# Second layer's begin in a two-layer decode kernel: where the rest of a kept V is put, and the order of the requests behind it

## The chip, the core and the metric

One core of a Trainium2 chip runs the whole program. The metric is the time on the device in microseconds (us), the median of several runs; a profiled execution gives a trace with the span and the records of each engine: PE (matmuls), DVE, ACT, POOL, SP (SyncE, which here only asks for transfers), and the 16 DMA engines.

## The reference

One token passes attention with a cache of 4096 positions and an MLP, and the same two blocks once more with the same weights and caches.

```
def _A_ref(x, k_cache, v_cache, wq, wo):
    q = (x @ wq) as 32 heads of 128
    scores = einsum("bhqd,bhkd->bhqk", q, k_cache) * (Dh ** -0.5)
    p = softmax(scores)
    o = einsum("bhqk,bhkd->bhqd", p, v_cache)
    return o @ wo                      # wq 512 x 4096, wo 4096 x 512

def _B_ref(x, w1, b1, w2, b2):
    return gelu(x @ w1 + b1) @ w2 + b2 # 512 -> 1376 -> 512

x = x + A(layernorm(x));  x = x + B(layernorm(x))
x = x + A(layernorm(x));  x = x + B(layernorm(x))
```

All is float32. K and V are 64 MiB each and are read in both layers, except for what is kept.

## The kernel before

The 32 heads are taken in 8 groups of four (`G`, `J`). A group's K is 8 MiB, in 8 chunks of 1 MiB (`C`); a chunk is 2048 columns (`NC`) of the 128 partitions. V is cut likewise. One tile, `arena` (line 74), holds nearly everything; places in it are told here in slots of `NC` columns, 0 to 27. Slots 0 to 23 take three blocks of 8 MiB in turn; `SPARE` is slot 19.75, `HELD` 22.75, `PAIR` 25.44 (two chunks: a wo and a wq). A `load` (line 76) is one request on SP's queue; the requests stay in the order of the program, and each waits until the last readers of its place are done. SP runs them one after the other, so a waiting one holds all behind it.

The first layer takes the groups 0 to 7, the second 7 to 0, so the second layer starts with data that are still there. Call its first three turns of the loop (line 380, n = 0, 1, 2; groups 7, 6, 5) stage one, two and three, with K7, V7, K6, V6, K5, V5.

A stage: `scores` (line 199; 4 MATMULs a chunk, which the trace shows as 8 passes), `softmax` (line 204: DVE takes the maximum, ACT the exponential, PE turns the result at line 213), `values` (line 227; 8 passes a chunk), `scaled_out` (line 232), `head_out` (line 254, the product with wo), `queries` (line 188: DVE four steps at lines 190 and 192, PE four products at line 194). `idle` (line 356) is a filler: a MATMUL whose result nobody reads. Fillers stand before the change in the last stage of each layer (`FILL` = 3 behind the scores and some more) and in the MLP.

What lies where when the second layer begins:

- K7 in slots 0 to 7, V7 in 8 to 15, all there.
- V6's first 3.75 chunks in slots 16 to 19.75, and 1.25 more in five PSUM banks (`pK`). The rest, 3 MiB, was overwritten by weights and is loaded again.
- K6 goes to `SPARE` + 1 and + 2 (chunks 0, 1), `PAIR` + 1 (chunk 2), and slots 0 (chunk 3) and 1 to 4 (chunks 4 to 7, one request), as K7's chunks are scored.
- V6's chunks 3 to 7 are put together in slots 6 to 10: its rest is loaded to slots 8 to 10 once V7's chunks there are used, and ACT copies the kept part to slots 6 and 7 (lines 413, 416).
- The weights of the next stages go to `PAIR`; then K5 in two halves to slots 12 to 15 and 16 to 19; then V5 to 0 to 7.
- Stage one's softmax writes to slot 5 (`p`), and the turned values (`ot`) right behind it (`free_now`, line 98).

A stage's PE work is emitted by a scheduler, which sets the order on PE, DVE and ACT; fillers and requests keep their place.

Of the kernel before, what the change touches and what calls it, by code (L numbers as in the profile page):

```python
# [23 lines left out]
C = 8  # L24
# [3 lines left out]
U = 512  # L28
KEPT = 5
NC = 4 * U  # L30
BLOCK = 8 * NC

STAY = 3 * NC + 3 * U
# [2 lines left out]
PAIR = HELD + 4 * FJ * J  # L36
ARENA = PAIR + 2 * NC
SMALLS = 240
PITCH = 1024
W2_PARTS = ((0, 4), (4, 8), (8, FB)), ((0, 6), (6, 9), (9, FB))  # L40
HIDDEN = ((0, 4), (4, 8), (8, FB))
# [10 lines left out]
def decode_layers(ctx: ExitStack, tc: tile.TileContext, x, k, v, w, w1, b1, w2, b2, out):  # L52
# [23 lines left out]
    def load(at, src):  # L76
        t = arena[:, at : at + src.shape[-1]]
        tc.keep_in_program_order(nc.sync.dma_start(t, src))
        return t
# [4 lines left out]
    def chunk(t, i=0):  # L84
        return t[:, NC * i : NC * (i + 1)].rearrange("p (j n) -> p j n", j=4)
# [12 lines left out]
    def free_now(layer, n):  # L98

        if layer == 0:  # L100
            at = HELD + 2 * NC
        elif n == 0:
            at = 5 * NC
        else:
            at = SPARE + NC if n < 3 else 2 * BLOCK + NC
        return arena[:, at : at + U], arena[:, at + U : at + U + 4 * 129]
# [120 lines left out]
    def values(i, pt, vt, c, of=C):  # L227
        for j in range(J):
            nc.tensor.matmul(pO[32 * j : 32 * j + 4, :], pt[:, j, c, :], by_head(vt)[:, j],  # L229
                             start=(i == 0), stop=(i == of - 1))  # L230
# [114 lines left out]
    def stream(what, g, pieces, base):  # L345

        for a, b in pieces:
            t = load(base + NC * a, part(k if what == "k" else v, g, a, b))
            for c in range(a, b):
                here[what, g, c] = chunk(t, c - a)  # L350
                yield c, here[what, g, c]
# [7 lines left out]
    for layer in range(2):  # L359
        order = list(range(G)) if layer == 0 else list(range(G))[::-1]  # L360
        if layer == 0:
            nm, ss, xc = mean_of(xs, s, pB[:, P : P + 1])
            z = queries(0, xc, wq_first, pO)
        else:
            for c in range(4):
                query_block(c, xs, wq_first)
                if c == 1:
                    nm, ss, xc = mean_of(xs, s, pB[:, P : P + 1])
        if layer == 1:
            here["k", order[1], 2] = chunk(load(PAIR + NC, part(k, order[1], 2, 3)))  # L370
            negm = small("negm")
            nc.vector.tensor_copy(negm, nm)
            z = first_queries(negm)
        xc_l = small("xc_l", 4)
        r = rstd_of(ss, pB[:, P + 1 : P + 2])
        nc.vector.tensor_copy(xc_l, xc)
        sc, nsc = small("sc"), small("nsc")
        nc.vector.tensor_scalar(sc, r, DH ** -0.5, None, op0=ALU.mult)
        nc.vector.tensor_scalar(nsc, r, -(DH ** -0.5), None, op0=ALU.mult)
        for n, g in enumerate(order):  # L380
            first, final = n == 0, n == G - 1

            k_home, v_home = ((2 * n + i) % 3 * BLOCK for i in (1, 2))
            if layer == 1:
                k_home, v_home = 12 * NC if n == 2 else BLOCK, 0

            if layer == 1 and n == 0:
                tiles = [(c, here["k", g, c]) for c in range(C)]
            elif layer == 1 and n == 1:
                tiles = [(c, here["k", g, c]) for c in range(3)]  # L390
                tiles += list(stream("k", g, ((3, 4), (4, 8)), -3 * NC))
            else:
                halves = first or (layer == 1 and n == 2)
                tiles = stream("k", g, LAST_K if final else HALVES if halves else WHOLE, k_home)
            for c, t in tiles:
                scores(z, c, t)
                if layer == 0 and final and c == LAST_K[0][1] - 1:
                    load(HELD, w1[:, : W1_AT[1]])
            if final:
                for _ in range(FILL):  # L400
                    idle(t, pO)
            p, ot = free_now(layer, n)
            pt, rl = softmax(sc, nsc, p)
            if layer == 1 and n == 0:
                z = queries(n + 1, xc_l, wq_next, pH)

            if layer == 1 and n == 0:
                for c in range(C):
                    values(c, pt, here["v", g, c], c)
            elif layer == 1 and n == 1:  # L410
                at, n_kept = 6 * NC, STAY + U * KEPT
                load(at + n_kept - 3 * NC, v[g][:, n_kept:BLOCK])
                nc.scalar.copy(arena[:, at : at + STAY - 3 * NC], arena[:, SPARE - STAY + 3 * NC : SPARE])
                for i in range(KEPT):
                    to = at + STAY - 3 * NC + U * i
                    nc.scalar.copy(arena[:, to : to + U], pK[i])
                for c in range(C):
                    values(c, pt, here["v", g, c] if c < 3 else chunk(arena[:, at:], c - 3), c)
            elif final:
                last_v = chunk(arena[:, v_home + BLOCK - NC : v_home + BLOCK])  # L420
                for c, t in stream("v", g, LAST, v_home):
                    values(c, pt, t, c, C - 1)
                    if c == C - 2:
                        others = scaled_out(rl, ot)
                    if c > 0:
                        idle(t, pS)
                for a in (BLOCK - NC, BLOCK - NC // 2):
                    load(v_home + a, v[g][:, a : a + NC // 2])
                for c in range(C):
                    here["v", g, c] = chunk(arena[:, v_home + NC * c : v_home + NC * (c + 1)])  # L430
            else:
                for c, t in stream("v", g, WHOLE, v_home):
                    for i in range(KEPT):
                        if layer == 0 and n == G - 2 and c == (STAY + U * i) // NC:
                            nc.scalar.copy(pK[i], t[:, STAY // U % J + i - J * (c - STAY // NC), :])
                    values(c, pt, t, c)

            if layer == 1 and n == 0:
                wo_t = chunk(arena[:, PAIR : PAIR + NC])
            elif final:  # L440
                at = PAIR + NC * layer
                for a, b in WO_PARTS:
                    load(at + U * a, of_w(wo_at(g), 1)[:, U * a : U * b])
                wo_t = chunk(arena[:, at : at + NC])
                if layer == 0:
                    load(HELD + W1_AT[1], w1[:, W1_AT[1] : W1_AT[2]])
                for a, b in W2_PARTS[layer]:
                    load(SPARE + U * a, w2[:, U * a : U * b])
                    if layer == 0 and a == 0:
                        load(HELD + W1_AT[2], w1[:, W1_AT[2] :])  # L450
            else:
                t = load(PAIR, of_w(wo_at(g) if layer == 0 else wq_at(g - 1), 2))
                wo_t, wq_next = (chunk(t, i) for i in ((0, 1) if layer == 0 else (1, 0)))
            on = scaled_out_last(rl, pt, last_v, others) if final else scaled_out(rl, ot)
            if final:
                idle(last_v, pO, 256)
            head_out(on, wo_t, n)
            if final:
                idle(last_v, pO, 256)
            if not final and not (layer == 1 and n == 0):  # L460
                z = queries(n + 1, xc_l, wq_next, pO, ot[:, :U] if layer == 0 and n == G - 2 else None)
            if n == G - 2:
                row_to_quadrants(p)
        at = work.tile([P, P], F32, name="pt")
        nc.vector.transpose(at, pW)
        x1, s1 = set_x(of_32(at, 4), 1.0, xs[:, :, 0])
        if layer == 0:
            xb = small("xb", 4)
        else:

            ends = arena[:, 2 * BLOCK : 2 * BLOCK + 3 * P]
            xb = of_32(ends, 4)
        mlp(x1, s1, w1_t, w2_t, xb, *((None, last_v) if layer == 0 else (ends, None)))
        if layer == 0:
            mt = work.tile([P, P], F32, name="pt")
            nc.vector.transpose(mt, pM)
            xs, s = set_x(of_32(mt, 4), 0.5, xb)
            g = G - 2
            wq_first = wq_next
            wq_next = chunk(load(SPARE, of_w(wq_at(g), 1)))  # L480
            for c in range(2):
                here["k", g, c] = chunk(load(SPARE + NC * (c + 1), part(k, g, c, c + 1)))
# [44 lines left out]
```

## Time and profile before

| | |
|---|---|
| median of 3 runs | 684.21 us (682.26 to 685.05) |
| the profiled execution's own time | 686.15 us |
| its span | 684.4 us |
| mean granted PE clock in it | 0.792 |
| PE busy | 416.6 us (61%) |
| DVE busy | 117.8 us (17%) |
| ACT busy | 23.0 us (3%) |
| read from HBM | 286.47 MB, 419 GB/s over the span |

A line of a timeline has the start in the span, the duration, engine, line of the kernel, operation, output <- input, shape and number; in brackets the idle time before it and what ended it. "SPq" is SP's queue: its rows are requests, and their duration is that of the issue, not of the transfer. "PEclk" or "clock" is the granted share of PE's clock.

### The profile page before, as it was taken

The numbers are of one execution on the slowest core, as the hardware profiler recorded it, in microseconds if no ns is written. First come the engines' busy times: TensorE is split into PE (matmuls) and PEld (weight loads), VectorE is DVE, ScalarE is ACT, GpSimd is POOL, SyncE is SP. The second block draws the span as 40 slices with busy tenths as digits, with TensorE's granted clock in tenths as the row PEclk, the third lists the DMA queues.
The fourth block names the chain that finished last, engine by engine and source line by source line (L and its number), as shares of the span: only waits on it lengthen the run. The fifth ranks groups of instructions, "written<-read, shape, count | busy, mean of one in ns | idle before, by whom it ended". The sixth has DMA issues, their size and how long they took to land.

```text
span 684.4 us, 6615 instructions
## 1 busy us (share of the span) xinstructions
PE 416.6 (61%) x2938; PEld 108.8 (16%) x2938; DVE 117.8 (17%) x390; ACT 23.0 (3%) x50; POOL 4.8 (1%) x22
## 2 busy tenths in 40 slices
PE   2644664555544856559597888454475554955786
PEld 1111110111100111112024222110011111211113
DVE  3002120121201202012114212120120201203113
ACT  0000000000000000001000200000000000000000
POOL 0000000000000000000001000000000000000000
PEclk9868676687777876769898798777787776787999
DMA  8999999999999999999999989999999999999996
GB/s 368 429 438 445 457 429 426 426 432 426 429 430 418 452 437 430 429 412 428 420 416 377 370 337 428 458 426 429 410 453 430 433 429 417 447 444 411 420 414 256
DMA packets 12852, 286.89 MB, mean 419 GB/s; under 512 B 1812, under 2 KB 1816, under 8 KB 3608
## 3 DMA queue, kind: packets, MB, share of 16 engines
q1 hardware_dynamic: 12392, 286.47, 98.1%
q8 instruction: 23, 0.38, 0.2%
q10 hardware_dynamic: 432, 0.01, 0.0%
q14 instruction: 5, 0.04, 0.0%
HBM read 286.47 MB, written 0.00 MB: 419 GB/s over the span
## 4 chain that ended last, share of the span: by engine, by line
DMA 45%; PE 35%; another core or an unknown queue 13%; DVE 4%; ACT 1%; issue 1%; SPq 0%; ACTq 0%; DVEq 0%
DMA arena<-in_k 28%; PE pS L201 16%; PE pO L229 11%; DMA arena<-in_w 10%; DMA arena<-in_v 7%; PE pB L257 5%; PE pO L194 1%; PE pO L213 1%; ACT arena L211 1%; DVE arena L233 1%; DMA xcol<-in_x 1%; DVE mx L205 1%; DVE arena L192 1%; DVE mb L209 0%
## 5 line engine op out<-in xcount | busy, mean ns | idle before, releaser
L201 PE MATMUL pS<-arena,zq 128*8 128x512 f32 x1024 | 148.6, 725 | 103.1 <-DMA arena<-in_k 102.7
L229 PE MATMUL pO<-arena,pt 128*4 128x512 f32 x1008 | 144.1, 714 | 88.7 <-DMA arena<-in_v 87.4
L201 PEld LDWEIGHTS pS<-arena,zq 128*8 128x8 f32 x1024 | 28.3, 102 | 214.7 <-DMA arena<-in_k 115.9
L257 PE MATMUL pB<-arena,smalls 128*1 128x512 f32 x112 | 57.0, 657 | 7.0 <-DVE smalls L238 7.0
L205 DVE TENSOR_REDUCE mx<-pS 128x1 f32<-128x512 f32 x16 | 11.1, 691 | 289.3 <-PE pS L201 289.3
L229 PEld LDWEIGHTS pO<-arena,pt 128*4 128x4 f32 x1008 | 27.6, 96 | 192.5 <-issue 180.4
L213 PE MATMUL pO<-ident,arena 128*128 128x128 f32 x64 | 15.1, 379 | 39.7 <-ACT arena L211 39.7
L192 DVE SCALAR_TENSOR_TENSOR arena<-arena,smalls 128x512 f32<-128x512 f32 x45 | 33.8, 751 | 1.6
L211 ACT ACTIVATE arena<-pS,smalls 128x512 f32<-128x512 f32 x16 | 12.4, 778 | 549.0 <-DVE smalls L210 548.9
L190 DVE TENSOR_SCALAR arena<-arena,smalls 128x512 f32<-128x512 f32 x15 | 7.3, 486 | 128.2 <-DMA arena<-in_w 128.2
L233 DVE STREAM_TRANSPOSE arena<-pO 128x512 f32<-128x512 f32 x16 | 11.5, 717 | 73.9 <-PE pO L229 73.9
L194 PE MATMUL pO<-one,arena 128*128 128x1 f32 x112 | 15.5, 260 | 11.7 <-DVE arena L233 9.5
L213 PEld LDWEIGHTS pO<-ident,arena 128*128 128x128 f32 x64 | 9.7, 188 | 54.0 <-ACT arena L211 47.7
L194 PEld LDWEIGHTS pO<-one,arena 128*128 128x128 f32 x112 | 14.4, 201 | 23.8 <-DVE arena L233 19.7
L257 PEld LDWEIGHTS pB<-arena,smalls 128*1 128x1 f32 x112 | 8.9, 89 | 45.5 <-issue 35.1
L357 PE MATMUL pS<-arena,ident 128*8 128x512 f32 x30 | 15.2, 592 | 0.0
L357 PE MATMUL pO<-arena,ident 128*8 128x512 f32 (+1 forms) x20 | 9.8, 613 | 0.0
L335 PE MATMUL pO<-arena,smalls 128*1 128x128 f32 x176 | 6.1, 272 | 3.7 <-DVE smalls L309 1.4
L217 DVE STREAM_TRANSPOSE smalls<-ls 128x32 f32<-128x32 f32 x16 | 3.4, 214 | 17.7 <-ACT arena L211 17.7
L155 PE MATMUL pB<-smalls,negmean 128*128 128x1 f32 x8 | 2.1, 337 | 7.0 <-DVE smalls L150 6.4
L215 DVE COPY pt<-pO 128x128 f32<-128x128 f32 x16 | 4.5, 278 | 4.4 <-PE pO L213 4.4
L335 PEld LDWEIGHTS pO<-arena,smalls 128*1 128x1 f32 x176 | 4.0, 83 | 6.4 <-issue 2.1
(94 smaller groups left out, 103.0 us busy)
## 6 DMA issues: line engine op xcount, KB each, us to landing
arena<-in_k SPq DMA_DIRECT2D x7, 4096.0 KB, 17.9
arena<-in_w SPq DMA_DIRECT2D x13, 2048.0 KB, 33.4
arena<-in_v SPq DMA_DIRECT2D x10, 1024.0 KB, 25.9
arena<-in_k SPq DMA_DIRECT2D x8, 1024.0 KB, 11.1
arena<-in_w SPq DMA_DIRECT2D x6, 1024.0 KB, 11.8
arena<-in_k SPq DMA_DIRECT2D x2, 2048.0 KB, 21.9
arena<-in_v SPq DMA_DIRECT2D x2, 2048.0 KB, 24.2
arena<-in_v SPq DMA_DIRECT2D x1, 3072.0 KB, 9.8
```

Source lines behind the costliest of these rows:

```text
L190: nc.vector.tensor_scalar(t, wt[:, 0, :], xc[:, 0:1], None, op0=ALU.mult)
L192: nc.vector.scalar_tensor_tensor(t, wt[:, c, :], xc[:, c : c + 1], t, op0=ALU.mult, op1=ALU.add)
L194: nc.tensor.matmul(at[:, j : j + 1], t[:, P * j : P * (j + 1)], one, start=True, stop=True)
L201: nc.tensor.matmul(pS[32 * j : 32 * j + C, :], z[:, j, C - 1 - c : 2 * C - 1 - c], kt[:, j, :], start=(c == 0), stop=(c == C - 1))
L205: nc.vector.tensor_reduce(mx[:, 0:1], pS, axis=AX.X, op=ALU.max)
L211: nc.scalar.activation(p, pS, AF.Exp, bias=bias[:, 0:1], scale=sc, accum_out=ls[:, 0:1])
L213: nc.tensor.transpose(pT[:, b].rearrange("p j r -> p (j r)"), p[:, P * b : P * (b + 1)], ident)
L229: nc.tensor.matmul(pO[32 * j : 32 * j + 4, :], pt[:, j, c, :], by_head(vt)[:, j], start=(i == 0), stop=(i == of - 1))
L233: nc.vector.transpose(ot[:, :512], pO)
L257: nc.tensor.matmul(pB[0:1, :], on[:, d : d + 1], wt[:, d, :], start=n == 0 and d == 0, stop=n == G - 2 and d == 3)
L335: pin(nc.tensor.matmul(pM[32 * j : 32 * j + 1, :], g[:, c - b0 : c - b0 + 1], w2_t[c][:, P * j : P * (j + 1)], start=(c == 0), stop=(c == ...
L357: pin(nc.tensor.matmul(at[:C, :n], ident[:, :C], t[:, 0, :n], start=True, stop=True))
```

## The change

Five edits, all at the passage from the first layer to the second:

1. V6's chunks 3 to 7 go to slots 8, 9, 5, 6, 7. The rest of V6 is loaded in two requests, chunks 6 and 7 to slots 6 and 7 and chunk 5 to slot 5, which are places of K7 and of stage one's `p`, no longer of V7. ACT copies the kept part in eight pieces of 512 columns to slots 8 and 9. Stage one's `ot` moves to slot 11.
2. K6's chunks 4 to 7 are three requests: 4, 5, and 6 with 7.
3. The requests of V6's rest stand ahead of the scores of stage two in the program.
4. K5's first half is asked for ahead of the weights; it was behind them.
5. Fillers: three behind stage one's scores, one at the end of the first layer's MLP.

```diff
 ARENA = PAIR + 2 * NC
 SMALLS = 240
+K2_HOME = 12 * NC
...
         elif n == 0:
             at = 5 * NC
+            return arena[:, at : at + U], arena[:, 11 * NC : 11 * NC + 4 * 129]
...
             if layer == 1:
-                k_home, v_home = 12 * NC if n == 2 else BLOCK, 0
+                k_home, v_home = K2_HOME if n == 2 else BLOCK, 0
...
                 tiles = [(c, here["k", g, c]) for c in range(3)]
-                tiles += list(stream("k", g, ((3, 4), (4, 8)), -3 * NC))
+                tiles += list(stream("k", g, ((3, 4), (4, 5), (5, 6), (6, 8)), -3 * NC))
+
+                at = [None] * 3 + [8 * NC, 9 * NC, 5 * NC, 6 * NC, 7 * NC]
+                n_kept = STAY + U * KEPT
+                load(at[6], v[g][:, 6 * NC : BLOCK])
+                load(at[n_kept // NC] + n_kept % NC, v[g][:, n_kept : 6 * NC])
+                for u in range(3 * NC, n_kept, U):
+                    to = at[u // NC] + u % NC
+                    nc.scalar.copy(arena[:, to : to + U], arena[:, SPARE - STAY + u : SPARE - STAY + u + U]
+                                   if u < STAY else pK[(u - STAY) // U])
+                for c in range(3, C):
+                    here["v", g, c] = chunk(arena[:, at[c] : at[c] + NC])
+            elif layer == 1 and n == 2:
+                tiles = [(c, here["k", g, c]) for c in range(4)]
+                tiles += list(stream("k", g, ((4, 8),), k_home))
             else:
-                halves = first or (layer == 1 and n == 2)
-                tiles = stream("k", g, LAST_K if final else HALVES if halves else WHOLE, k_home)
+                tiles = stream("k", g, LAST_K if final else HALVES if first else WHOLE, k_home)
...
-            if final:
+            if final or (layer == 1 and first):
                 for _ in range(FILL):
                     idle(t, pO)
...
             elif layer == 1 and n == 1:
-                at, n_kept = 6 * NC, STAY + U * KEPT
-                load(at + n_kept - 3 * NC, v[g][:, n_kept:BLOCK])
-                nc.scalar.copy(arena[:, at : at + STAY - 3 * NC], arena[:, SPARE - STAY + 3 * NC : SPARE])
-                for i in range(KEPT):
-                    to = at + STAY - 3 * NC + U * i
-                    nc.scalar.copy(arena[:, to : to + U], pK[i])
                 for c in range(C):
-                    values(c, pt, here["v", g, c] if c < 3 else chunk(arena[:, at:], c - 3), c)
+                    values(c, pt, here["v", g, c], c)
+
+                for _ in stream("k", order[2], ((0, 4),), K2_HOME):
+                    pass
...
         if layer == 0:
+            idle(last_v, pS)
             mt = work.tile([P, P], F32, name="pt")
```

SP's queue at the passage, from wq of stage two and K6 on (a chunk is 128x2048, so 128x8192 is half a K). Before:

```order
L78 DMA arena<-in_w 128x2048
L78 DMA arena<-in_k 128x2048 x4
L78 DMA arena<-in_k 128x8192
L78 DMA arena<-in_v 128x6144
L78 DMA arena<-in_w 128x4096
L78 DMA arena<-in_k 128x8192 x2
L78 DMA arena<-in_v 128x16384
L78 DMA arena<-in_w 128x4096
```

In the changed kernel, whose lines count one or two higher:

```order
L79 DMA arena<-in_w 128x2048
L79 DMA arena<-in_k 128x2048 x6
L79 DMA arena<-in_k 128x4096
L79 DMA arena<-in_v 128x4096
L79 DMA arena<-in_v 128x2048
L79 DMA arena<-in_k 128x8192
L79 DMA arena<-in_w 128x4096
L79 DMA arena<-in_k 128x8192
L79 DMA arena<-in_v 128x16384
L79 DMA arena<-in_w 128x4096
```

K6's last half is cut in three, V6's rest in two, and K5's first half stands ahead of the weights.

PE from the end of the first layer's MLP (L335) through stage one to stage two's scores (L201 with `zq_95`). Before:

```order
L335 MATMUL pO<-arena,smalls 1x128 x28
L175 MATMUL pO<-arena,smalls 2x128 x8
L155 MATMUL pB<-smalls,negmean 128x1
L175 MATMUL pO<-arena,smalls 2x128 x8
L155 MATMUL pB<-smalls,negmean 128x1
L201 MATMUL pS<-arena,zq_94 8x512 x32
L194 MATMUL pB<-one,arena 128x1 x4
L213 MATMUL pO<-ident,arena 128x128 x4
L201 MATMUL pS<-arena,zq_95 8x512
L229 MATMUL pO<-arena,pt 4x512 x32
L201 MATMUL pS<-arena,zq_95 8x512 x8
L257 MATMUL pB<-arena,smalls 1x512 x4
```

In the changed kernel:

```order
L337 MATMUL pO<-arena,smalls 1x128 x28
L359 MATMUL pS<-arena,ident 8x512
L177 MATMUL pO<-arena,smalls 2x128 x8
L157 MATMUL pB<-smalls,negmean 128x1
L177 MATMUL pO<-arena,smalls 2x128 x8
L157 MATMUL pB<-smalls,negmean 128x1
L203 MATMUL pS<-arena,zq_94 8x512 x32
L359 MATMUL pO<-arena,ident 8x512 x3
L215 MATMUL pO<-ident,arena 128x128 x4
L196 MATMUL pB<-one,arena 128x1 x4
L231 MATMUL pO<-arena,pt 4x512 x32
L203 MATMUL pS<-arena,zq_95 8x512 x5
```

The fillers (L359) are new; the queries' four products (L194, now L196) moved behind the transposes, and the first scores of stage two behind all of stage one's values.

ACT from the first layer's MLP (the last L313) to stage two's softmax (the last row, which also counts those that follow). Before:

```order
L313 ACTIVATE smalls<-smalls 128x3
L413 COPY arena<-arena 128x1536
L416 COPY arena<-pK_86 128x512
L416 COPY arena<-pK_87 128x512
L416 COPY arena<-pK_88 128x512
L211 ACTIVATE arena,ls<-pS,smalls 128x512
L416 COPY arena<-pK_89 128x512
L416 COPY arena<-pK_90 128x512
L211 ACTIVATE arena,ls<-pS,smalls 128x512 x7
```

In the changed kernel:

```order
L315 ACTIVATE smalls<-smalls 128x3
L213 ACTIVATE arena,ls<-pS,smalls 128x512
L401 COPY arena<-arena 128x512 x3
L401 COPY arena<-pK_86 128x512
L401 COPY arena<-pK_87 128x512
L401 COPY arena<-pK_88 128x512
L401 COPY arena<-pK_89 128x512
L401 COPY arena<-pK_90 128x512
L213 ACTIVATE arena,ls<-pS,smalls 128x512 x7
```

The exponential of stage one now stands ahead of all copies. On DVE one row of the queries' first step (L190 before) moves ahead of the row that writes stage one's queries (L183 before).

## The prediction

> **What bounds the kernel now.** I read the page's line of the rate first: what the transfers moved in each of 40 slices of 17.1 us.
>
> ```profile
> GB/s 368 429 438 445 457 429 426 426 432 426 429 430 418 452 437 430 429 412 428 420 416 377 370 337 428 458 426 429 410 453 430 433 429 417 447 444 411 420 414 256
> ```
>
> It lies near 430 almost everywhere; the dip is at slices 22 to 24 (377, 370, 337), 359 to 411 us, where the second layer begins. Next the chain of work that ended last, in order of time (start us, us, what):
>
> ```profile
> 427.62 3.66 PE pS L201 x32
> ...
> 431.30 43.83 DMA arena<-in_k
> ...
> 483.81 34.92 DMA arena<-in_k
> ...
> 644.90 22.24 DMA arena<-in_v
> ...
> 667.15 13.49 DMA arena<-in_w
> ```
>
> From 431 us to the end each link is a transfer issued long before it was needed: the 8 MiB asked for at 431.30 land 43.8 us later, over twice what they take alone. The queue is always full there, so whatever is gained before 431 us reaches the end undiminished, and nothing else does. Windows of the trace (start:end us, us, busy time of PE, PEld, DVE, ACT and POOL, then clock, DMA share, GB/s) show the holes:
>
> ```profile
> 392.00:396.00 4.00, 4.00 (x37) 1.18 (x33) 0.00 (x0) 0.00 (x0) 0.00 (x0) 0.88 0.40 102
> 400.00:404.00 4.00, 4.00 (x28) 0.85 (x27) 0.00 (x0) 0.00 (x0) 0.00 (x0) 1.00 0.69 295
> 404.00:408.00 4.00, 3.72 (x30) 0.70 (x25) 0.19 (x1) 0.00 (x0) 0.00 (x0) 1.00 0.90 328
> 440.00:600.00 160.00, 88.27 (x524) 20.43 (x524) 23.43 (x65) 2.61 (x6) 0.00 (x0) 0.74 1.00 431
> ```
>
> 102, 295 and 328 GB/s against 431: the queue ran dry. PE is busy all through them: SyncE cannot ask because PE has not yet left the buffers. The requests (time, us to issue), and below them, in the same order, size and us from issue to landing:
>
> ```profile
> 376.15 0.33 SPq L78 DMA_DIRECT2D arena<-in_k  x1
> 381.25 0.33 SPq L78 DMA_DIRECT2D arena<-in_k  x1
> 394.07 0.33 SPq L78 DMA_DIRECT2D arena<-in_v  x1
> 403.51 0.33 SPq L78 DMA_DIRECT2D arena<-in_w  x1
> 417.28 0.33 SPq L78 DMA_DIRECT2D arena<-in_k  x1
> ```
>
> ```profile
> arena<-in_k SPq DMA_DIRECT2D x1, 1024.0 KB, 7.1
> arena<-in_k SPq DMA_DIRECT2D x1, 4096.0 KB, 12.4
> arena<-in_v SPq DMA_DIRECT2D x1, 3072.0 KB, 9.8
> arena<-in_w SPq DMA_DIRECT2D x1, 2048.0 KB, 7.1
> arena<-in_k SPq DMA_DIRECT2D x1, 4096.0 KB, 14.3
> ```
>
> Landings: K6's chunk 3 at 383.25, its rest at 393.65, V6's rest at 403.87, the weights at 410.6, K5's second half at 431.58. V6's rest was asked for at 394.07, after the landing before it, and the weights 0.4 us before one: two dry queues.
>
> **What the change can win at most.** Between 383.25 and 431.58 the same 17 MiB land before and after (K6 4, V6 3, weights 2, K5 8), in 48.3 us. At 431 GB/s a MiB takes 2.44 us and 17 take 41.5 us. So **6.9 us** is the most. Slow transfers before 383 (K6's chunks 0 to 3) aren't touched.
>
> **What decides how much comes.** PE's rows at the place (time, us, line, operation, passes, [idle before]):
>
> ```profile
> 371.61 0.62 PE L175 MATMUL pO<-arena,smalls 128*2 128x128 f32 x16 [0.80 <-DVE smalls L150]
> ...
> 374.20 9.55 PE L201 MATMUL pS<-arena,zq 128*8 128x512 f32 x64 [0.18 <-DVE zq L183]
> 383.69 1.05 PE L194 MATMUL pB<-one,arena 128*128 128x1 f32 x8
> 386.86 1.11 PE L213 MATMUL pO<-ident,arena 128*128 128x128 f32 x4 [2.12 <-ACT arena L211]
> ...
> 388.37 1.03 PE L229 MATMUL pO<-arena,pt 128*4 128x512 f32 x3
> ...
> 389.17 8.68 PE L229 MATMUL pO<-arena,pt 128*4 128x512 f32 x60
> ...
> 412.05 9.40 PE L229 MATMUL pO<-arena,pt 128*4 128x512 f32 x64 [0.38 <-DVE pt L215]
> ...
> 650.70 2.74 PE L357 MATMUL pO<-arena,ident 128*8 128x512 f32 x6
> 653.64 0.66 PE L213 MATMUL pO<-ident,arena 128*128 128x128 f32 x4 [0.20 <-ACT arena L211]
> ```
>
> In the new order c4, c5, c6-7 of K6 wait for the scores of stage one chunk by chunk; V6's chunks 6-7 lie in K7's slots 6 and 7 (last score), V6's chunk 5 in slot 5 (transposes of stage one, L213). These are free by 388 us even at the old pace: 7 MiB, enough until 383.25 + 17.1 = 400.3. K5's first half needs the end of stage one's values; on a dry queue 3 MiB needed 9.8 us where streaming takes 7.3, so a request must come 2.5 us ahead: by 397.8, about when the values end at the old pace (397.85, the row at 389.17). The weights need stage two's first three chunks scored: far ahead of 407. K5's **second half** overwrites V6's kept chunks 0 to 2, so it waits for three chunks of stage two's values, as before. It was issued at 417.28; with 2.5 us and 9.8 us for its 4 MiB it would land at 429.6, and the full queue wants it at 383.25 + 41.5 = 424.7. Call d the us by which PE reaches those values earlier: the gain is the smaller of 6.9 and **2.0 + d**. V5 after it needs all of stage two's values (the row at 412.05 ends at 421.5, less d), which is ahead of 424.7 - 2.5 if d is at least 0.
>
> **What PE gains (d).** The clock, in windows as above:
>
> ```profile
> 369.04:372.46 3.42, 1.74 (x46) 1.19 (x42) 0.49 (x3) 0.00 (x0) 0.00 (x0) 1.00 0.85 330
> 372.46:379.29 6.83, 6.65 (x45) 1.82 (x48) 3.92 (x14) 0.00 (x0) 0.67 (x1) 0.50 0.97 354
> 382.70:386.11 3.41, 2.04 (x20) 1.07 (x12) 1.58 (x6) 3.11 (x5) 0.00 (x0) 1.00 0.83 346
> 386.11:392.94 6.83, 6.08 (x28) 1.86 (x29) 1.12 (x6) 1.66 (x4) 0.00 (x0) 0.50 0.91 387
> 406.59:410.00 3.41, 1.13 (x6) 0.09 (x1) 1.51 (x5) 0.37 (x1) 0.00 (x0) 1.00 1.04 447
> ```
>
> PE was busy for 1.74 of 3.42 us, and for the next 6.83 us the clock was 0.50; again after 2.04 of 3.41. Two rows of DVE and ACT, for below:
>
> ```profile
> 374.14 0.49 DVE L190 TENSOR_SCALAR arena<-arena,smalls 128x512 f32<-128x512 f32 x1
> ...
> 384.33 1.55 ACT L416 COPY arena<-pK 128x512 f32<-128x512 f32 x3
> ```
>
> - *One filler at layer one's end.* A filler is two passes of 2.74 / 6 = 0.46 us; it lies in the idle 0.80 us ahead of L175 (at worst 0.1 us late) and lifts that window to 2.6 of 3.4 busy. If the clock then stays, stage one's 64 score passes take about 7.1 us (twice the 32 passes in 3.66, less one pipeline end) instead of 9.55: **2.4 us**.
> - *Three fillers behind the scores.* 2.74 us at full clock, ahead of the transposes; the queries' products (L194, 1.05) move behind these, so from the last score to the first value stand 2.74 + 0.66 + 1.05 and small waits, 4.6 us; before it was 383.75 to 388.37, 4.6 too: **0**. In the last stage the same filler ends 0.2 us before the transposes can start.
> - *Stage one's values* then run at full clock: about 7.1 us, where they stretch from 388.37 to some 398 with eight score passes between, that now follow: **2.1 us**.
> - *Act's copies* leave the front of the softmax (0 to 0.3) and become eight of 512 columns, about 0.5 us each by the row above, after the first values, long before 412: hidden; without that cover 4 us.
> - *DVE* does the first step of the next queries (0.49) before stage one's queries are written; the second half of L175 at full clock gives about that back: 0, between -0.5 and +0.2.
>
> d = 2.4 + 0 + 2.1 = **4.5 us**; stage two's softmax stays unfilled, and its values slow (9.40, the row at 412.05). Gain: 2.0 + 4.5 = **6.5 us**, just below the 6.9 cap.
>
> The Trainium skill, "TensorE: Matmul & The Clock Gate", Part 1, speaks against the fillers: it puts the fall of the clock after a whole idle window of some 3.4 us. Here no gap is that long (0.80 and 2.12 us in the rows above) and yet the clock fell twice: the trace disagrees. Its word that the window runs free of the kernel agrees with falls at different points of similar stages.
>
> *Three more transfers.* A piece of 1 MiB costs nothing beside a full queue and something beside a short one:
>
> ```profile
> 342.00:354.00 12.00, 11.17 (x72) 2.54 (x71) 0.36 (x2) 0.00 (x0) 0.00 (x0) 1.00 1.01 416
> 368.00:384.00 16.00, 14.13 (x160) 4.99 (x159) 4.64 (x19) 1.04 (x1) 0.67 (x1) 0.79 0.92 344
> ```
>
> Pieces of 1 MiB land in both windows, the queue full in the first. At 344 GB/s the three new pieces would take 9.1 us, 1.8 more than at 431; at 416, 0.3. I take 0, as they are asked for 4 us and more ahead, and keep 1.8 as the end. SyncE's own issue (0.33 us each) lies in its waits.
>
> The profiled execution took 686.15 us (span 684.4): by this sum 679.65. It lies 1.9 us above the median of the runs, 684.21; so 684.21 - 6.5 = **677.7 us**.
>
> **The rivals.**
>
> 1. *Only one filler works* (phase of the clock's window, or passes that don't count as activity). d is 2.1 to 2.4, the gain 4.1 to 4.4: about 680.0. For it: the windows that lost the clock were 33, 51 and 60% busy, which says from below alone where the limit lies.
> 2. *The clock falls as before.* d = 0, the stall moves from V6 to K5's second half, gain 2.0: 682.2. Here the change does in effect half of what it says: the order is new, the pace of PE is not. The Trainium skill's rule of the whole idle window (same page and part) would give this case. Against it: the last stage's fillers, with full clock through 650.70 and 653.64.
> 3. *Slower: fillers at half clock.* If the clock falls as the fillers begin, six passes take about 5.1 us instead of 2.74, in a softmax that left 3.1 between the last score and the transposes: 2.0 late, and the queries' products behind the transposes add 1.05. d = -3.1, gain -1.1: 685.3. It decides from d = -2.0 on. Against it: they begin after 64 unbroken passes.
> 4. *Small transfers cost their own price.* Gain 6.5 - 1.8 = 4.7: 679.5. The Trainium skill, "DMA: Bandwidth & Descriptors", Anatomy of one DMA, gives about 2.0 us fixed per transfer (GpSimd's path); for three as an estimate 6, a gain of 0.5. The 416 GB/s disagree while the queue is full.
>
> **How the numbers follow.** Forecast 0.62, rival 1 0.17, rival 2 0.11, rival 3 0.05, rival 4 0.05. A measurement of this kernel tells about 0.5%, 3.4 us, from no change. Faster by over that: 0.62, the most of rivals 1 and 4, 0.13 together: 0.75. Within: rival 2, the rest of 1 and 4, and most of 3: 0.22. Slower by over 0.5%: 0.03. The runs of before lie from 682.26 to 685.05. The range goes down to the cap of 6.9 from a median 1.9 lower, 675.4, and up to rival 2, 682.4.
>
> **What would show it.** Right: no window from 392 to 408 far below 431 GB/s; clock 1.00 from 372 to 393; V6's last chunk landed by 401; K5's second half asked for by 413 and landed by 425.5; from there the old chain 6 to 7 us earlier. Wrong: clock 0.50 in either stretch, a hole ahead of K5's second half near 415, slow pieces between 383 and 400, or a later request that comes late after all.

## The result, and the profile after

| | before | after |
|---|---|---|
| median | 683.94 us (682.26 to 686.37, 6 runs) | 680.24 us (680.10 to 681.78, 6 runs) |
| after / before | | 0.9947, 95% interval 0.9926 to 0.9967 |
| the profiled execution, own time | 686.15 us | 680.21 us |
| its span | 684.4 us | 678.3 us |

The medians differ by 3.7 us, the two profiled executions by 5.9 us (spans 6.1). Both numbers are right, and the gap between them is what this case is about. The forecast was 677.7 us, in a range of 675.4 to 682.4.

First the changed kernel's page, the rate in 40 slices of 17.0 us:

```profile
GB/s 371 433 434 433 434 433 433 422 444 434 433 434 416 450 433 434 433 433 403 425 415 387 408 438 449 433 430 433 424 435 430 433 433 406 454 433 414 421 416 260
```

About two thirds of the dip is gone: 387 and 408 are left in slices 22 and 23, where before 377, 370 and 337 stood in slices 22 to 24, against the usual 431 or so. Then the three windows in which before had its holes, and the windows of the clock (columns as before: busy times of the engines, clock, DMA share, GB/s):

```profile
392.00:396.00 4.00, 4.00 (x26) 0.81 (x18) 1.13 (x3) 0.00 (x0) 0.00 (x0) 1.00 1.01 432
400.00:404.00 4.00, 2.73 (x22) 0.49 (x17) 1.07 (x4) 0.00 (x0) 0.00 (x0) 1.00 1.03 444
404.00:408.00 4.00, 2.02 (x12) 0.68 (x16) 1.44 (x8) 0.87 (x2) 0.00 (x0) 0.80 1.01 434
368.86:372.27 3.41, 2.37 (x50) 1.08 (x42) 0.48 (x3) 0.00 (x0) 0.00 (x0) 1.00 0.85 304
382.51:385.93 3.42, 3.18 (x23) 1.66 (x25) 1.57 (x9) 0.87 (x2) 0.00 (x0) 1.00 1.03 434
...
372.00:393.00 21.00, 20.19 (x190) 6.47 (x179) 6.85 (x27) 4.95 (x10) 0.92 (x1) 1.00 1.01 410
374.00:426.00 52.00, 46.27 (x342) 12.04 (x346) 12.73 (x41) 5.82 (x12) 0.92 (x1) 0.97 1.03 433
```

432, 444 and 434 GB/s where 102, 295 and 328 stood. The two windows with fillers are busy for 2.37 and 3.18 us (1.74 and 2.04 before), and over the whole of 372 to 393 the clock is 1.00. PE's rows of stage one and two (time, us, line, passes):

```profile
374.18 7.05 PE L203 MATMUL pS<-arena,zq 128*8 128x512 f32 x64 [0.57 <-DVE smalls L171]
381.05 2.74 PE L359 MATMUL pO<-arena,ident 128*8 128x512 f32 x6
384.03 0.66 PE L215 MATMUL pO<-ident,arena 128*128 128x128 f32 x4 [0.24 <-ACT arena L213]
384.52 0.95 PE L196 MATMUL pB<-one,arena 128*128 128x1 f32 x8
385.40 7.05 PE L231 MATMUL pO<-arena,pt 128*4 128x512 f32 x64
...
406.63 8.61 PE L231 MATMUL pO<-arena,pt 128*4 128x512 f32 x64 [0.42 <-DVE pt L217]
```

Stage one's scores take 7.05 us (9.55 before), its values 7.05, and stage two's values begin at 406.63 instead of 412.05. SP's requests, and in the same order their size and us to landing:

```profile
383.82 0.33 SPq L79 DMA_DIRECT2D arena<-in_v  x1
384.75 0.33 SPq L79 DMA_DIRECT2D arena<-in_v  x1
392.51 0.33 SPq L79 DMA_DIRECT2D arena<-in_k  x1
398.52 0.33 SPq L79 DMA_DIRECT2D arena<-in_w  x1
411.07 0.33 SPq L79 DMA_DIRECT2D arena<-in_k  x1
```

```profile
arena<-in_v SPq DMA_DIRECT2D x1, 2048.0 KB, 14.6
arena<-in_v SPq DMA_DIRECT2D x1, 1024.0 KB, 16.2
arena<-in_k SPq DMA_DIRECT2D x1, 4096.0 KB, 18.1
arena<-in_w SPq DMA_DIRECT2D x1, 2048.0 KB, 17.2
arena<-in_k SPq DMA_DIRECT2D x1, 4096.0 KB, 14.4
```

Each is asked for ahead of need: it lands 14 to 18 us later, and of these a full queue, at 2.44 us a MiB, spends 2.4 to 9.8 us on its own bytes. V6's last chunk lands at 384.75 + 16.2 = 400.9, K5's second half at 411.07 + 14.4 = 425.5, before at 431.6. From there to the end of the span it is 252.8 us in both (684.4 - 431.6 and 678.3 - 425.5). So in these two executions the whole difference arises ahead of 431 us, as forecast.

### The profile page after: what moved, and what is told of

It reads as the page before. It is cut to its first block, busy times and chain, and to the rows that moved or that the text cites. A ratio compares the mean times of both kernels' runs of the same rounds, so it can differ in the third digit from the quotient of the medians.

```text
span 678.3 us, 6637 instructions
## 1 busy us (share of the span) xinstructions
PE 409.8 (60%) x2946; PEld 106.6 (16%) x2946; DVE 116.9 (17%) x390; ACT 23.2 (3%) x52; POOL 5.0 (1%) x22
## 4 chain that ended last, share of the span: by engine, by line
DMA 51%; PE 32%; another core or an unknown queue 10%; DVE 4%; issue 1%; ACT 1%; SPq 0%; ACTq 0%; DVEq 0%
DMA arena<-in_v 33%; PE pO L231 15%; DMA arena<-in_w 9%; PE pS L203 9%; DMA arena<-in_k 8%; PE pB L259 4%; PE pO L196 1%; ACT arena L213 1%; DMA xcol<-in_x 1%; PE pO L337 1%; DVE mx L207 1%; PE pO L215 1%; DVE arena L194 1%; DVE arena L235 1%
## 5 line engine op out<-in xcount | busy, mean ns | idle before, releaser
L203 PE MATMUL pS<-arena,zq 128*8 128x512 f32 x1024 | 141.7, 704 | 101.5 <-DMA arena<-in_k 100.7
L231 PE MATMUL pO<-arena,pt 128*4 128x512 f32 x1008 | 139.7, 707 | 94.3 <-DMA arena<-in_v 92.8
L259 PE MATMUL pB<-arena,smalls 128*1 128x512 f32 x112 | 58.7, 674 | 7.0 <-DVE smalls L240 7.0
L215 PE MATMUL pO<-ident,arena 128*128 128x128 f32 x64 | 12.8, 332 | 38.3 <-ACT arena L213 38.3
L194 DVE SCALAR_TENSOR_TENSOR arena<-arena,smalls 128x512 f32<-128x512 f32 x45 | 33.8, 751 | 1.5
L213 ACT ACTIVATE arena<-pS,smalls 128x512 f32<-128x512 f32 x16 | 12.4, 777 | 555.2 <-DVE smalls L212 555.2
L196 PE MATMUL pO<-one,arena 128*128 128x1 f32 x112 | 15.6, 260 | 11.9 <-DVE arena L235 9.7
L196 PEld LDWEIGHTS pO<-one,arena 128*128 128x128 f32 x112 | 14.4, 201 | 24.0 <-DVE arena L235 19.9
L215 PEld LDWEIGHTS pO<-ident,arena 128*128 128x128 f32 x64 | 8.2, 164 | 53.3 <-ACT arena L213 48.1
L359 PE MATMUL pS<-arena,ident 128*8 128x512 f32 x32 | 16.2, 592 | 0.0
L359 PE MATMUL pO<-arena,ident 128*8 128x512 f32 (+1 forms) x26 | 10.6, 526 | 0.0
L198 DVE COPY zq<-pO 128x4 f32<-128x4 f32 x14 | 2.3, 165 | 14.4 <-PE pO L196 14.4
```

What stands on the lines that cost most here:

```text
L194: nc.vector.scalar_tensor_tensor(t, wt[:, c, :], xc[:, c : c + 1], t, op0=ALU.mult, op1=ALU.add)
L196: nc.tensor.matmul(at[:, j : j + 1], t[:, P * j : P * (j + 1)], one, start=True, stop=True)
L203: nc.tensor.matmul(pS[32 * j : 32 * j + C, :], z[:, j, C - 1 - c : 2 * C - 1 - c], kt[:, j, :], start=(c == 0), stop=(c == C - 1))
L213: nc.scalar.activation(p, pS, AF.Exp, bias=bias[:, 0:1], scale=sc, accum_out=ls[:, 0:1])
L215: nc.tensor.transpose(pT[:, b].rearrange("p j r -> p (j r)"), p[:, P * b : P * (b + 1)], ident)
L259: nc.tensor.matmul(pB[0:1, :], on[:, d : d + 1], wt[:, d, :], start=n == 0 and d == 0, stop=n == G - 2 and d == 3)
```

## The experiments

All numbers are medians with the range and the number of runs; the ratio stands against runs of the kernel before on the same chip. Those runs had medians of 683.6, 683.6 and 683.3 us in the three groups of experiments.

**The kernel before, profiled three more times** (no edit; labels b_again, b_third, b_fourth). What was open: the first profile of before was 2.2 us over the median, so was its hole the usual one?

> The kernel before, unchanged, profiled once more. Theory (PE's clock sets the holes, and its windows fall differently from one execution to the next; the first profile of before was an unlucky one): from the landing of K5's second half to the end of the span it is again 252.8 us (431.58 to 684.4 before, 425.46 to 678.3 after), so the span's distance from 678.3 is the lateness of that landing; the executions spread over 3 us or more, with the higher mean clock in the shorter spans, median near 684. Rival (the change costs about 2 us somewhere behind 431 us that the two single profiles hide): the landing comes at 431.6 in this profile too and the stretch behind it is shorter than 252.8.

> The kernel before, a third profile. Theory: the stretch from the landing of K5's second half to the end is 252.8 to 253.4 us again, whatever the span (679.5 to 684.5); V6's rest is asked for at 390 to 394, and the later it is asked for the longer the span. Rival: the spans differ behind 431 us.

> The kernel before, a fourth profile, expected as the third: 252.8 to 253.4 us behind the landing of K5's second half, and a span that follows V6's request.

Measured: b_again 683.46 us (681.91 to 685.17, 12), ratio 0.9992 (0.9977 to 1.0007); the single runs 683.32 and 685.10. Two windows of each profile, first of the first profile of before, then of b_again, b_third, b_fourth:

```profile
372.00:393.00 21.00, 18.70 (x130) 5.88 (x125) 6.62 (x26) 4.76 (x8) 0.67 (x1) 0.67 0.95 375
374.00:426.00 52.00, 45.15 (x289) 11.63 (x288) 13.25 (x41) 5.63 (x10) 0.67 (x1) 0.82 0.93 379
```

```profile
372.00:393.00 21.00, 18.54 (x169) 5.67 (x163) 6.49 (x26) 4.76 (x8) 0.65 (x1) 0.92 1.00 406
374.00:426.00 52.00, 43.42 (x328) 11.22 (x320) 12.82 (x40) 5.63 (x10) 0.65 (x1) 0.97 1.01 419
```

```profile
372.00:393.00 21.00, 18.55 (x161) 6.55 (x157) 6.61 (x26) 4.76 (x8) 0.65 (x1) 0.84 1.00 401
374.00:426.00 52.00, 45.01 (x308) 12.81 (x312) 13.26 (x42) 5.63 (x10) 0.65 (x1) 0.87 0.97 402
```

```profile
372.00:393.00 21.00, 18.70 (x161) 5.76 (x157) 6.50 (x26) 4.77 (x8) 0.67 (x1) 0.84 1.01 395
374.00:426.00 52.00, 44.59 (x330) 11.47 (x329) 13.34 (x43) 5.64 (x10) 0.67 (x1) 0.95 0.98 400
```

The same program had a mean clock of 0.67, 0.92, 0.84 and 0.84 in these 21 us, and 379, 419, 402 and 400 GB/s; after has 433 in the second window (shown above). K5's second half, asked for and landed:

| profile | span | asked for | landed | from landing to end | clock, 372 to 393 |
|---|---|---|---|---|---|
| before, first | 684.4 | 417.28 | 431.6 | 252.8 | 0.67 |
| b_again | 680.0 | 410.41 | 427.2 | 252.8 | 0.92 |
| b_third | 681.5 | 414.61 | 428.6 | 252.9 | 0.84 |
| b_fourth | 683.2 | 411.76 | 430.3 | 252.9 | 0.84 |
| after | 678.3 | 411.07 | 425.5 | 252.8 | 1.00 |

The stretch behind the landing is constant: the rival (a hidden loss behind 431 us) falls. The theory stands in its first part: the spans of the kernel before differ by what the queue lost in this place. K5's second half lands 1.7, 3.1, 4.8 and 6.1 us later than in after, 3.9 in the mean, close to the 3.7 between the medians.

The second part, that the span follows V6's request, holds only roughly: b_third and b_fourth asked for V6's rest at the same time (391.42 and 391.34) and differ by 1.7 us, since in b_fourth K6's rest had landed 2.3 us later already. Nor does the clock alone order the spans: over 374 to 426 it was 0.95 in b_fourth and 0.87 in b_third, and b_fourth is the longer one. The first profile was the unluckiest of the four: between 372 and 417 us it lost the clock three times for 6.8 us each (from 372.5, 386.1 and 410.0); b_third lost it twice for 6.8, b_fourth twice and b_again once for 3.4. Its deepest hole, 102 GB/s in 392 to 396 where V6's rest came late, is hardly there in the other three (369, 350 and 342 GB/s). They lose most behind it, at the weights: 287 GB/s in 398 to 402 in b_again, 199 and 229 in 400 to 404 in b_third and b_fourth.

**Without any filler** (no_fill): the change's places and order alone.

```diff
-            if final or (layer == 1 and first):
+            if final:
...
-            idle(last_v, pS)
```

> The change without its four fillers. Theory: the stream before 410 is full, but K5's second half is asked for when PE has used V6's chunk 2, at about 417.3 if the clock falls twice as in the first profile of before, so it lands at 429.6 and the span is about 682.4; if PE is luckier by 2 us, 680.4. Median 681.5 to 684, spread above 1 us. Rival (the new order alone is what helped, the fillers are decoration): 680.2 with a spread of 0.5, as after.

Measured: 681.58 us (680.79 to 682.10, 7), ratio 0.9970 (0.9955 to 0.9985), within the theory's numbers. In its profile the clock fell at 383 and 407, and the hole stands exactly where rival 2 of the prediction put it, ahead of K5's second half (window, then the request and its time to landing):

```profile
412.00:416.00 4.00, 4.00 (x32) 0.79 (x28) 0.00 (x0) 0.00 (x0) 0.00 (x0) 0.76 0.72 246
```

```profile
414.36 0.33 SPq L79 DMA_DIRECT2D arena<-in_k  x1
```

```profile
arena<-in_k SPq DMA_DIRECT2D x1, 4096.0 KB, 12.4
```

246 GB/s, and 12.4 us for 4 MiB on a queue about to run dry (the weights landed at 415.4, 1.0 us after the request), against 12.3 reckoned (2.5 and 9.8).

**The fillers alone** (fill_only): the kernel before with the two edits of fillers, places and order as before.

```diff
-            if final:
+            if final or (layer == 1 and first):
...
         if layer == 0:
+            idle(last_v, pS)
```

> The kernel before with the four fillers alone; places and order of the requests as before. Theory: with PE some 4 us earlier V6's rest is asked for at about 389 (before: 394.07), ahead of the 391 at which the queue needs it; the weights at about 399.5 come about 1 us late; K5's second half at about 412. Median 680.5 to 681.5, spread below 1 us: most of the gain without any new place or order. Rival (places and order are needed): holes near 393 and 403 stay, median 682 to 684.

Measured: 681.24 us (680.50 to 682.80, 12), ratio 0.9971 (0.9960 to 0.9982). The median is as the theory had it; the spread, 2.3 us, is not. V6's rest was asked for at 388.66 and left no hole; the one hole is at the weights:

```profile
398.00:402.00 4.00, 4.00 (x38) 0.79 (x26) 0.00 (x0) 0.00 (x0) 0.00 (x0) 1.00 0.80 270
```

```profile
398.10 0.33 SPq L78 DMA_DIRECT2D arena<-in_w  x1
```

```profile
arena<-in_w SPq DMA_DIRECT2D x1, 2048.0 KB, 9.2
```

They cannot be asked for before stage two's third chunk is scored, 398.1, and land at 407.3; behind V6's rest (400.3) a full queue would have had them at 405.2.

**One of the two fillers left out** (no_first without the single one, no_three without the three).

```diff
 no_first:
-            idle(last_v, pS)
 no_three:
-            if final or (layer == 1 and first):
+            if final:
```

> The change without the single filler at the first layer's end; the three behind stage one's scores stay. Theory: the clock falls at about 372 for 6.8 us, PE loses 2.4 us against after, K5's second half is asked for at 413.5 instead of 411.07, some 1.3 us after the queue needs it: span 679.5 to 680, median 681 to 682. Rival (this filler does nothing): the clock stays at 1.00 and the median is 680.2.

> The change without the three fillers behind stage one's scores; the single one stays. Theory: the clock falls behind stage one's softmax for 3.4 or 6.8 us, PE loses 1 to 3 us, K5's second half is asked for at 412 to 414.5 and lands at 425.5 to 427: median 680.8 to 681.8, as without any filler (681.58). Rival (either filler is enough): 680.2.

Measured: no_first 680.39 us (679.99 to 681.13, 6), ratio 0.9950 (0.9936 to 0.9965); no_three 681.25 us (680.67 to 682.95, 12), ratio 0.9967 (0.9954 to 0.9980). For the single filler the theory missed: its loss was forecast at 0.8 us or more and none can be told. For the three it hit in the number. The window in which the single filler would lie, in no_first:

```profile
368.61:372.02 3.41, 1.74 (x60) 1.16 (x53) 0.49 (x3) 0.00 (x0) 0.00 (x0) 1.00 0.87 303
372.00:393.00 21.00, 20.43 (x191) 6.60 (x184) 7.21 (x27) 4.96 (x10) 0.65 (x1) 1.00 1.01 408
```

1.74 us busy, the same as in the first profile of before, and here the clock stayed. In its own profile, of one of its faster runs (680.79), no_three kept the clock as well (window 382.31 to 385.73, busy 1.50 of 3.42 us). Two of its twelve runs near 682.9 suggest that it doesn't always, which no profile here shows: that the three fillers earn their 1.0 us by the clock is argued, not shown.

**K6's last half in one request** (k6_whole).

```diff
-                tiles += list(stream("k", g, ((3, 4), (4, 5), (5, 6), (6, 8)), -3 * NC))
+                tiles += list(stream("k", g, ((3, 4), (4, 8)), -3 * NC))
```

> The change with K6's chunks 4 to 7 in one request again. Theory: it is asked for when chunk 4 is scored, 378.7 at full clock, ahead of the 381 at which the queue needs it: no hole, median 680.2, within 0.4. Rival (the three transfers earn something of their own): a hole at 381 to 383 as before, 0.5 us or more.

Measured: 680.26 us (680.03 to 680.87, 6), ratio 0.9953 (0.9936 to 0.9969). As the theory had it: asked for at 378.59, the 4 MiB left no hole. The three requests neither cost nor earn anything that can be told.

**The weights ahead of K5's first half** (w_first), as in the kernel before.

```diff
-                for _ in stream("k", order[2], ((0, 4),), K2_HOME):
-                    pass
...
-                tiles = [(c, here["k", g, c]) for c in range(4)]
-                tiles += list(stream("k", g, ((4, 8),), k_home))
+                tiles = stream("k", g, HALVES, k_home)
```

> The change with the weights ahead of K5's first half again. Theory: the weights can be asked for at 398.5 alone, when stage two's third chunk is scored, and the queue needs them at 398.4; K5's first half follows at once. With PE as in after that is a hole of 0 to 2 us (the fillers alone lost 2 us at this place, asked 0.3 us late), one for one more where PE is later: median 680.3 to 682, spread above 1. Rival (this order is not what counts): 680.2 with a spread of 0.5.

Measured: 681.33 us (680.71 to 681.55, 11), ratio 0.9966 (0.9955 to 0.9978): 1.1 us over after, with a window of 293 GB/s at 398 to 402 where the weights wait. The median fits the theory, the spread of 0.8 is below what it had.

**Eight fillers instead of three** (eight): PE later, all else as in after.

```diff
-                for _ in range(FILL):
+                for _ in range(FILL if final else 8):
```

> The change with eight fillers instead of three behind stage one's scores: PE is made about 4.0 us later, at full clock. Theory (gain the smaller of 6.9 and 2.0 + d, d now 0.6): the queue stays full up to the weights, K5's second half is asked for at 415.1 and lands at 427.4, 1.9 us later than in after: median 682.2. Rival one (the queue is full anyway): 680.2. Rival two (PE's chain sets the end, each us counts): 684.2.

Measured: 682.04 us (680.57 to 683.67, 12), ratio 0.9980 (0.9968 to 0.9993), against 682.2 by the formula, 680.2 and 684.2 by the rivals. The median hit; the steps to it hit only in part. The profiled execution was one of the faster ones (681.77), and PE's clock did not fall in it at all between 374 and 426, so that K5's second half was asked for at 413.33, 1.8 us earlier than forecast; but it took 13.6 us instead of 12.3. The hole is again ahead of it:

```profile
412.00:416.00 4.00, 4.00 (x40) 0.96 (x36) 0.00 (x0) 0.00 (x0) 0.00 (x0) 1.00 0.81 274
```

**Fillers and the one swap** (v_old): the kernel before with the fillers and with K5's first half ahead of the weights; V6's rest, K6's requests and ACT's copies as before.

```diff
 (on top of fill_only)
                     values(c, pt, here["v", g, c] if c < 3 else chunk(arena[:, at:], c - 3), c)
+                for _ in stream("k", order[2], ((0, 4),), 12 * NC):
+                    pass
...
+            elif layer == 1 and n == 2:
+                tiles = [(c, here["k", g, c]) for c in range(4)]
+                tiles += list(stream("k", g, ((4, 8),), k_home))
             else:
-                halves = first or (layer == 1 and n == 2)
+                halves = first
```

> The kernel before with the four fillers and with K5's first half ahead of the weights; V6's rest and K6 stay as before. Theory: V6's rest is asked for at 388.7, 2 us ahead of need, K5's first half at 393.5, 4 us ahead, the weights at 398.1, long ahead; the queue is full and the time is that of after, 680.3, within 0.4, spread below 1. Rival (V6's new place and K6's three requests earn something): 680.8 or more, a hole near 393.

Measured: 679.96 us (679.84 to 681.51, 9), ratio 0.9953 (0.9937 to 0.9970): not to be told from after. One run lay 1.5 us higher, so the spread is wider than expected. The queue is full over the whole stretch, also where V6's rest still waits for V7:

```profile
374.00:426.00 52.00, 45.06 (x346) 13.47 (x344) 12.48 (x39) 5.53 (x10) 0.92 (x1) 1.00 1.03 438
...
398.00:402.00 4.00, 4.00 (x34) 0.79 (x26) 0.00 (x0) 0.00 (x0) 0.00 (x0) 1.00 1.04 449
```

**Fillers in stage two as well** (two_fill).

```diff
-            if final or (layer == 1 and first):
+            if final or (layer == 1 and n < 2):
```

> The change with three fillers behind stage two's scores too. Theory: the queue is full already; K5's second half is asked for at about 409.5 instead of 411.07 and lands no earlier than 425.3: median 680.2, within 0.3 of after. Rival (PE still sets the end): 0.5 to 1.5 us less.

Measured: 680.68 us (680.00 to 681.44, 12), ratio 0.9964 (0.9950 to 0.9978). K5's second half was asked for at 409.57, 1.5 us earlier than in after, and landed at 425.8: nothing earned, as the theory had it; if anything 0.4 us more, just outside what it allowed.

## Why the prediction was right, and where it was off

Direction and mechanism held; the size was 6.5 us forecast and 3.7 measured.

- *What bounds the kernel.* Right. The stretch behind the landing of K5's second half is 252.8 or 252.9 us in all four profiles of before and in after, whatever came ahead of it. In the profiles of the other experiments it is 252.9 to 253.4. The queue is full there, and the time is decided by what it lost before.
- *6.9 us at most.* Held for that execution: the landing moved by 6.1 us. The 17 MiB took 42.0 us (383.5 to 425.5) instead of the 41.5 reckoned.
- *The gain is the smaller of 6.9 and 2.0 + d.* Supported from several sides: with d made small (eight) the median is 682.04 against 682.2; without fillers the hole moves to K5's second half; with PE earlier still (two_fill) nothing more comes. Its lead of 2.5 us is too small in two profiles. In eight K5's second half was asked for 1.8 us ahead of the landing before it and landed 2.0 us after the time of a full queue, where 0.7 were reckoned; the last section has the other, fill_only.
- *d = 4.5 us.* Right in kind, 0.9 too small: stage two's values begin 5.4 us earlier (406.63 instead of 412.05). The scores of stage one gave 2.5 us (forecast 2.4), its values about 2.0 (forecast 2.1). The softmaxes, put at 0, gave 0.4 each: in stage one 4.2 us from the last score to the first value (381.23 to 385.40) instead of 4.6, and in both the transposes took 0.66 us instead of 1.11. K5's request came 6.2 us earlier, since stage two's clock, too, fell for 3.4 us instead of 6.8. ACT's copies ran behind the first values and were hidden.
- *One filler at layer one's end: 2.4 us.* Off. It is worth that only in an execution whose clock would fall at 372. Two of four profiles of before lost it there, the first for 6.8 us and b_fourth for 3.4; without this filler the median moved by 0.15 us, which isn't to be told from nothing.
- *Three more transfers: 0* (against rival 4). Right, as far as it was tried: k6_whole takes two of the three away and has 680.26 against 680.24; v_old has none of the three and 679.96.
- *The step that failed:* "It lies 1.9 us above the median of the runs, 684.21; so 684.21 - 6.5 = 677.7 us". The hole was measured in an execution that had lost the clock three times ahead of 417 us, the gain was taken off a median in which the hole is smaller. The 79 runs of before in all groups have a median of 683.5 and lie between 681.2 and 686.5; the profiled one, 686.15, is near the top. The other sum in the same paragraph, 686.15 - 6.5 = 679.65, was within 0.6 us of what was measured (680.21 for the profiled run, 680.24 for the median). It is the right kind of sum here, as the change doesn't shift the time: it takes it to a floor, that of the full queue, which is the same for lucky and unlucky executions. So the typical gain is the typical hole, 3.7 us, and the spread shrinks from 4.1 to 1.7 us (five of six runs within 0.5). That it came so near is in part luck: with d as measured the formula gives its cap, 6.9, and 679.25; the d that was too small and the cap that was too high nearly cancel. The forecast's 677.7 lies 2.5 us too low.
- *Rival 1* (only one filler works, about 680.0) came nearest in the number, but by the same sum from the median, and its mechanism isn't what the profile shows: the clock was 1.00 behind both places, and d was 5.4, not 2.1 to 2.4. What no_first adds is that the single filler was not needed in its profile, where the clock stayed without it; that it ever held the clock is not shown.
- *Rival 2* forecast 682.2 for places and order without the fillers' effect; no_fill has 681.58. *Rival 3* (slower) didn't occur: the fillers ran at full clock, 2.74 us, and ended 0.24 us before the transposes.

Which part earned what: fillers alone 2.4 us by the medians of their group, places and order alone 2.1, both 3.7, as each shortens the same hole. Of places and order it is the swap of K5's first half and the weights that counts next to the fillers (w_first loses 1.1 us); V6's new place and K6's three requests aren't needed beside these two (v_old).

## What to carry to other kernels

Where a transfer queue sets the time, look for the places where it runs dry, and ask of each which engine's progress holds the request back; making that engine earlier is worth time only up to the point where the queue stays full. A change that takes a kernel to such a floor must be forecast as a floor (the profiled execution's time less its own holes), not as a shift of the median: the profile shows the hole of one execution. Where PE's clock decides a hole, several profiles of the same kernel are needed before its size is known.

## What was not expected of the hardware

- The same PE work kept or lost its clock: 1.74 us busy in a window of 3.4 us was followed by 0.50 in the first profile of before (window from 369.04) and by 1.00 in no_first (from 368.61); 1.50 us kept it in no_three. The busy time of the trace alone doesn't say when the clock falls. The Trainium skill's "TensorE: Matmul & The Clock Gate", Part 1, has the windows run free of the program; the four profiles of one kernel, with clocks of 0.67 to 0.92 in the same 21 us, agree. Its whole idle window as the condition of a fall isn't borne out.
- A request that comes a little late can cost more than its lateness: in fill_only the weights were asked for 2.2 us ahead of the landing before them, 0.3 later than the 2.5 that were reckoned, and landed 2.1 us after the time of a full queue (405.2). The trace has 16 completion records for each of these requests, and the landing is the last of them. Fifteen of the 16 parts of the weights had landed by 405.5, 0.3 us late as reckoned; the sixteenth landed at 407.3.
- The same in b_fourth: fifteen parts of K6's rest had landed by 393.6, the sixteenth at 395.9 (in b_third 392.8 and 393.6). Such a lag is still there three requests later: the ninth of the 16 parts of K5's second half landed at 427.2 us in b_third and 427.3 in b_fourth, the last at 428.6 and 430.3. So the 1.7 us between these two spans stand between their slowest parts. Why a part falls behind stays open.
